# Retention attention and a two-layer MLP on one core: the MLP products in exact 12-bit pieces (three one-pass products) in place of Strassen on fp32, with half of the weights resident and two rounds over the token blocks

## The chip, the cores and the metric

The kernel runs on one core of a Trainium2 chip. The metric is the device time of one execution in microseconds (us); the kernel before takes 1010.7 us (median of three runs, 1009.96 to 1012.33). The engines are named as in the profile: PE is the matrix engine (PEld its weight loads), DVE the vector engine, ACT the scalar engine, POOL the GpSimd engine, SP the queue that issues most transfers. SBUF is the on-chip working memory, PSUM the small memory that PE writes into.

## The reference

Attention with decay for 8 batches and 8 heads, 576 positions, head size 64; its output, as 4608 tokens of 512 numbers, goes through a two-layer MLP with a PReLU between the layers.

```python
scores = q @ k^T / sqrt(64)
ret    = scores * Dmat                 # Dmat[i, j] = gamma_h ** (i - j) for i >= j, else 0
x      = (ret @ v) -> 4608 x 512
h = x @ w_in                           # 512 -> 2048
g = maximum(h, 0) + alpha * minimum(h, 0)
out = g @ w_out                        # 2048 -> 512, float32
```

The weights w_in and w_out reach the chip as float64 and are turned into float32 there. All products have to be good to fp32.

## The kernel before

Tokens are taken in 18 blocks of 256. The 2048 hidden channels are 8 units of 256. One unit of one block is the step that is repeated: h for 256 tokens and 256 channels, the PReLU, and that unit's share of the output. Blocks 0 and 1 use plain products while the weights still arrive (16 plain units); the other 16 blocks use Strassen's seven products of half-size operands (128 Strassen units). All matrices are fp32. Attention for a pair of heads is worked into the gaps between units: 28 pairs in this way, and the first batch in a form of its own at the start.

```python
def plain_unit(kb, i):                       # blocks 0 and 1
    for cc in range(NCC):                    # NCC = 4
        for x in range(2):
            nc.tensor.matmul(ph[:, x], w_in[...], xb[kb][:, cc], ...)      # L426, 256 columns
    ...
def mlp_unit(kb, i):                         # blocks 2 to 17
    for n, (m, o, l, r) in enumerate((... seven products ...)):
        for cc in range(2):
            nc.tensor.matmul(ph[m][:, o], w_in[i // UST][:, l, i % UST, cc], r[:, cc], ...)  # L470, 128 columns
    nc.scalar.copy(g[:, 7], ph[0][:, 2])
    for o, x0, x1 in (... four sums ...):
        nc.vector.tensor_tensor(out=o, in0=x0, in1=x1, op=ALU.add)         # L481, reads PSUM
    for m in range(2):
        nc.vector.tensor_scalar(g[:, 4 + 2 * m:6 + 2 * m], ..., ALU.min, ALU.mult)   # L484
    nc.vector.scalar_tensor_tensor(out=g[:, 0:4], ..., op0=ALU.max, op1=ALU.add)     # L486, both inputs in SBUF
    for o, x0, x1, op in (... four sums of g ...):
        nc.vector.tensor_tensor(out=g[:, o, :], in0=g[:, x0, :], in1=g[:, x1, :], op=op)   # L492, both in SBUF
    ...
def mlp_out(...):
    for n, (x, y) in enumerate(PROD):        # seven products
        nc.tensor.matmul(acc[kb][n // 2][:, n % 2, :], g[:, x, :], w_out[i][:, y, :], ...)  # L388, 256 columns
```

The weights stay on chip with their Strassen sums. Each piece of a weight (128 rows of 512 numbers; 32 pieces) is converted once from float64 while the plain blocks run. The intermediate c lies in PSUM.

```python
def piece_in(n):
    nc.scalar.activation(a, hi.bitcast(FP32), ACTF.Abs)
    nc.scalar.activation(lo, lo.bitcast(UINT32), ACTF.Copy, scale=2.0 ** -29)
def piece_out(n):
    c = ps_h.tile([P, 2, HM], INT32, tag="psh1", ...)                      # PSUM
    nc.vector.tensor_scalar(c.bitcast(FP32), a, HI_MIN, HI_MAX, ...)       # L307
    nc.vector.tensor_scalar(c, c, 3, 0x3FFFFFF8, ...)                      # L310
    nc.vector.scalar_tensor_tensor(out=dst, in0=hi, ..., in1=c, ...)       # L312
    nc.gpsimd.tensor_tensor(out=dst, in0=dst, in1=lo, op=ALU.add)          # L314
```

For a pair of heads ("joint", "pair_front", "running_sums", "pair_values") PE makes scores and states, DVE scales and masks the scores (four instructions, L636) and forms the running sums (L588 to L594), ACT copies the sums and q into the operands of the last product, POOL scales q (L531).

Of the kernel before, what the change touches and what calls it, by code (L numbers as in the profile page):

```python
# [10 lines left out]
FP32 = mybir.dt.float32  # L11
INT32 = mybir.dt.int32
UINT32 = mybir.dt.uint32
# [5 lines left out]
def kernel(  # L19
# [20 lines left out]
    NB = S // 32  # L40
# [3 lines left out]
    HM = DM // 2  # L44
    TB = 2 * P
    NKB = NTOK // TB
    NST = 4
    UST = NU // NST
    NRING = 6
# [3 lines left out]
    assert NPAIR == NCC and DM == 512 and NU % NST == 0 and TB % C == 0 and NB == 18  # L53
# [3 lines left out]
    wraw = ctx.enter_context(tc.tile_pool(name="wraw", bufs=3))  # L57
    ring = ctx.enter_context(tc.tile_pool(name="ring", bufs=1))
    xcomb = ctx.enter_context(tc.tile_pool(name="xcomb", bufs=2))
    nat = ctx.enter_context(tc.tile_pool(name="nat", bufs=2))  # L60
    attn = ctx.enter_context(tc.tile_pool(name="attn", bufs=1))
    mlp = ctx.enter_context(tc.tile_pool(name="mlp", bufs=3))
# [9 lines left out]


# [18 lines left out]


# [6 lines left out]

    def load_head(t, src, b, h):
        nc.sync.dma_start(t, src[b, h].rearrange("(j t) d -> t j d", t=C))

    def load_pair(n):
        b, c = pairs[n]
        kx, qx, kn = [nat.tile([P, S], FP32, tag=t, name=f"{t}_{n}") for t in ("kx", "qx", "kn")]
        kx, qx = [t.rearrange("p (n r) -> p n r", r=32) for t in (kx, qx)]  # L110
        kn = kn.rearrange("p (j d) -> p j d", d=D)
        vn = nat.tile([P, 2, NJ, D], FP32, tag="vn", name=f"vn_{n}")
# [5 lines left out]
        for h2 in range(2):  # L118

            nc.scalar.copy(vn[half(h2), h2, 0], zero[half(h2)])  # L120
# [3 lines left out]


    w_in = [wpool.tile([P, 7, UST, 2, P], FP32, tag=f"wi{i}", name=f"w_in{i}")
            for i in range(NST)]


    w_out = [wpool.tile([P, 7, HM], FP32, tag=f"wo{i}", name=f"w_out{i}") for i in range(NU)]  # L130


# [4 lines left out]

    def room(i, s0, n):
        return w_out[i][:, s0:s0 + n].rearrange("p s f -> p (s f)")
# [3 lines left out]
    part = [[room(i + 3 * (x % 2), 4 * (x // 2), 2 if x == 2 else 4).rearrange(  # L146
        "p (m h d) -> p m h d", h=H, d=D) for i in (2, 3, 4)] for x in range(2)]
    part.append([room(i, 4, 2).rearrange("p (m h d) -> p m h d", h=H, d=D) for i in (2, 3, 4)])
    sums = [[room(i, s0, 1).rearrange("p (c d) -> p c d", d=D) for i, s0 in x] for x in (
        ((5, 4), (5, 5), (5, 6), (6, 4)), ((6, 5), (6, 6), (7, 4), (7, 5)), ())]  # L150
    carry = [None] + [room(i, 6, 1).rearrange("p (c d) -> p c d", d=D) for i in (2, 7)]
# [28 lines left out]
    zero = const.tile([P, D], FP32, name="zero")  # L180
    nc.gpsimd.memset(zero, 0.0)
# [29 lines left out]
    th = const.tile([P, 4, H], FP32, name="th")  # L211
    nc.vector.scalar_tensor_tensor(out=tp[:, 0, 0], in0=pf[:, 1], scalar=float(D) ** -0.5,
# [5 lines left out]
    nc.vector.tensor_scalar(tp[:, 1], tp[:, 1], float(D) ** -0.5, None, ALU.mult)  # L218
# [3 lines left out]
    nc.vector.tensor_scalar(th[:, 0], pf[:, 1], float(D) ** -0.5, None, ALU.mult)  # L222
    nc.vector.reciprocal(pf[:, 1], pf[:, 1])
    nc.vector.tensor_tensor(out=th[:, 1], in0=pf[:, 1], in1=th[:, 2], op=ALU.mult)
    nc.vector.reciprocal(th[:, 3], th[:, 2])
# [4 lines left out]
    tabv = const.tile([P, NPAIR], FP32, name="tabv")  # L230
    for h2 in range(2):
        hd = slice(h2 * D, (h2 + 1) * D)
        nc.vector.tensor_copy(tabv[half(1 - h2)], th[half(1 - h2), 1, h2:H:2])
        nc.vector.tensor_copy(gch[hd, 0], th[hd, 2, h2:H:2])
        nc.vector.tensor_scalar(tabx[hd, :, 0], pf[hd, 0, h2:H:2], float(D) ** -0.5, None,
                                ALU.mult)
        nc.vector.scalar_tensor_tensor(out=tabx[hd, :, 1], in0=dif[hd, 5, h2:H:2], scalar=1.0,
                                       in1=tabx[hd, :, 0], op0=ALU.add, op1=ALU.mult)
    for i in range(2):
        nc.vector.tensor_tensor(out=gch[:, i + 1], in0=gch[:, i], in1=gch[:, i], op=ALU.mult)  # L240

    win32 = moe_w_in.bitcast(INT32).rearrange("(c p) (x f two) -> c p x f two", p=P, x=2, two=2)
# [784 lines left out]
```

## Time and profile before

| | before |
|---|---|
| time, median of three | 1010.7 us |
| profiled span | 1008.5 us |
| PE busy in 0 to 25 us, 25 to 50 us | 16.87, 23.81 us |
| DVE busy in 75 to 100 us, in 100 us from 300 us on | 22.88, 80.98 us |
| POOL busy in 125 to 150 us, in 100 us from 300 us on | 19.09, 9.10 us |
| moved between memory and chip | 64.30 MB, mean 64 GB/s |

How to read the profile: every instruction has a start and an end on its engine. Rows of groups give a count, the total busy time and the mean of one instruction. PE's instructions overlap (the end of one is modelled and reaches into the next), so a mean of PE is no rate; the distance from one start to the next is. An fp32 matmul shows as two records. In rows of the timeline, the first number is the start and the second the length of a run of like instructions.

### The profile page before, as it was taken

Reading aid. Unit: us, or ns where it says so; the run is one execution under the profiler, and the core shown is the slowest. Engines: PE = TensorE matmul, PEld = TensorE weight load, DVE = VectorE, ACT = ScalarE, POOL = GpSimd, SP = SyncE. Lnnn points to the kernel's source line nnn. Section 1 sums busy time; section 2 is a strip of 40 time slices with the busy share of each in tenths; the row PEclk is TensorE's granted clock in tenths of the full one; section 3 lists DMA queues with packets and bytes.
Section 4 is the critical chain, followed back from the end, with each engine's and each line's share of the span. In section 5 each row is a group of like instructions: output and inputs, shape, how many; then the busy total and the mean of one; then the engine's idle time right before and its main releaser. Section 6 shows DMA issues by size and latency. Waiting matters only on the chain.

```text
span 1008.5 us, 23133 instructions
## 1 busy us (share of the span) xinstructions
PE 995.2 (99%) x9389; PEld 891.9 (88%) x9389; DVE 773.4 (77%) x2086; ACT 267.3 (27%) x605; POOL 179.0 (18%) x201
## 2 busy tenths in 40 slices
PE   6999999999999999999999999999999999999998
PEld 5666668999999999999999999999999999999997
DVE  7769968887878778687777788878788776666665
ACT  5656652322222222022022121222222210000000
POOL 5656674210200020100020000200010001010000
PEclk9999999999999999999999999999999999999999
DMA  9986744232322222031122222323222000000000
GB/s 236 252 194 150 182 74 109 49 72 48 69 48 65 53 42 63 13 69 31 40 48 51 40 52 44 70 48 69 48 43 52 13 22 1 22 1 22 1 22 22
DMA packets 229595, 64.30 MB, mean 64 GB/s; under 512 B 214368, under 2 KB 223088, under 8 KB 229488
## 3 DMA queue, kind: packets, MB, share of 16 engines
q1 hardware_dynamic: 227088, 62.02, 27.4%
q8 instruction: 74, 1.21, 0.5%
q10 hardware_dynamic: 2400, 0.79, 0.4%
q14 instruction: 33, 0.27, 0.1%
HBM read 53.35 MB, written 9.44 MB: 62 GB/s over the span
## 4 chain that ended last, share of the span: by engine, by line
PE 98%; DMA 1%; issue 0%; DVE 0%; ACT 0%; SPq 0%; DVEq 0%
PE ph L470 40%; PE po L388 38%; PE ph L426 6%; PE po L405 6%; PE pv L652 3%; PE ps L616 1%; PE ps L622 1%; DMA w_out<-in_k_dram 1%; PE pv L966 1%; PE pt L695 0%; PE ps L714 0%; PE pv L773 0%; PE ps L559 0%; PE pu L734 0%; PE pu L577 0%
## 5 line engine op out<-in xcount | busy, mean ns | idle before, releaser
L388 PE MATMUL po<-w_out,g 128*128 128x256 f32 x1792 | 408.1, 379 | 0.0
L388 PEld LDWEIGHTS po<-w_out,g 128*128 128x128 f32 x1792 | 330.7, 190 | 39.7
L481 DVE TENSOR_TENSOR g<-ph,g 128x256 f32<-128x256 f32 (+1 forms) x512 | 187.0, 386 | 134.0 <-PE ph L470 67.7
L470 PE MATMUL ph<-xb,w_in 128*128 128x128 f32 x2048 | 272.7, 276 | 0.0
L470 PEld LDWEIGHTS ph<-xb,w_in 128*128 128x128 f32 x2048 | 257.1, 192 | 7.4 <-issue 0.5
L470 PE MATMUL ph<-xt,w_in 128*128 128x128 f32 x1536 | 213.3, 275 | 0.0
L470 PEld LDWEIGHTS ph<-xt,w_in 128*128 128x128 f32 x1536 | 192.1, 192 | 0.0
L476 ACT COPY g<-ph 128x128 f32<-128x128 f32 x128 | 34.1, 266 | 404.4 <-PE ph L470 391.9
L492 DVE TENSOR_TENSOR g<-g 128x128 f32<-128x128 f32 x512 | 129.4, 293 | 7.0
L531 POOL TENSOR_TENSOR qx<-qx,tabx 128x576 f32<-128x576 f32 x28 | 32.7, 1168 | 353.2 <-DMA qx<-in_q_dram 180.1
L486 DVE SCALAR_TENSOR_TENSOR g<-g 128x512 f32<-128x512 f32 x128 | 89.8, 701 | 3.0
L484 DVE TENSOR_SCALAR g<-g,alpha 128x256 f32<-128x256 f32 x256 | 85.8, 377 | 3.7
L405 PE MATMUL po<-w_out,g 128*128 128x512 f32 x128 | 58.6, 599 | 0.8 <-DVE g L442 0.8
L426 PE MATMUL ph<-xb,w_in 128*128 128x256 f32 x256 | 58.6, 383 | 0.0
L663 ACT COPY xb<-pv 128x256 f32<-128x256 f32 (+3 forms) x84 | 23.2, 315 | 126.5 <-PE pv L652 126.5
L426 PEld LDWEIGHTS ph<-xb,w_in 128*128 128x128 f32 x256 | 47.9, 190 | 9.3 <-issue 2.4
L600 ACT COPY vn<-su 64x512 f32<-64x512 f32 x56 | 34.5, 616 | 78.3 <-DVE su L594 77.9
L636 DVE SCALAR_TENSOR_TENSOR mt<-ps,th,mask 64x256 f32<-64x256 f32 x96 | 46.4, 483 | 2.2
L456 POOL TENSOR_TENSOR xt<-xb 128x256 f32<-128x256 f32 x16 | 11.6, 727 | 196.9 <-PE ph L470 196.9
L405 PEld LDWEIGHTS po<-w_out,g 128*128 128x128 f32 x128 | 23.4, 190 | 24.4 <-issue 22.8
L629 DVE SCALAR_TENSOR_TENSOR mt<-pv,th,mask 64x64 f32<-64x64 f32 x48 | 13.6, 283 | 40.2 <-ACT xb L663 39.8
L536 ACT ACTIVATE vn<-vn,tabv 64x576 f32<-64x576 f32 x56 | 43.2, 772 | 1.8 <-DMA vn<-in_v_dram 0.5
(136 smaller groups left out, 737.9 us busy)
## 6 DMA issues: line engine op xcount, KB each, us to landing
out_dram<-osb SPq DMA_DIRECT2D x34, 256.0 KB, 2.1
kx<-in_k_dram SPq DMA_DIRECT2D x112, 72.0 KB, 2.5
qx<-in_q_dram SPq DMA_DIRECT2D x112, 72.0 KB, 2.9
vn<-in_v_dram SPq DMA_DIRECT2D x56, 144.0 KB, 3.3
kn<-in_k_dram SPq DMA_DIRECT2D x56, 144.0 KB, 3.8
raw<-in_moe_w_in_dram SPq DMA_DIRECT2D x24, 256.0 KB, 4.4
raw<-in_moe_w_out_dram SPq DMA_DIRECT2D x10, 512.0 KB, 4.5
w_in<-in_moe_w_out_dram SPq DMA_DIRECT2D x6, 512.0 KB, 5.6
```

What stands on the lines that cost most here:

```text
L388: nc.tensor.matmul(acc[kb][n // 2][:, n % 2, :], g[:, x, :], w_out[i][:, y, :], start=(i == 0 and n % 2 == 0), stop=(i == NU - 1 and (n % ...
L405: nc.tensor.matmul(acc[kb][m], g[:, 2 * x + m], w_out[i][:, 2 * x:2 * x + 2].rearrange("p x f -> p (x f)"), start=(i == 0 and x == 0), sto ...
L426: nc.tensor.matmul(ph[:, x], w_in[i // UST][:, cc // 2 * 2 + x, i % UST, cc % 2], xb[kb][:, cc], start=(cc == 0 and x == 0), stop=(cc == N ...
L470: nc.tensor.matmul(ph[m][:, o], w_in[i // UST][:, l, i % UST, cc], r[:, cc], start=(n in (0, 3) and cc == 0), stop=(n in (2, 6) and cc == ...
L476: nc.scalar.copy(g[:, 7], ph[0][:, 2])
L481: nc.vector.tensor_tensor(out=o, in0=x0, in1=x1, op=ALU.add)
L484: nc.vector.tensor_scalar(g[:, 4 + 2 * m:6 + 2 * m], g[:, 2 * m:2 * m + 2], 0.0, alpha[:, fc:fc + 1], ALU.min, ALU.mult)
L486: nc.vector.scalar_tensor_tensor(out=g[:, 0:4].rearrange("p x t -> p (x t)"), in0=g[:, 0:4].rearrange("p x t -> p (x t)"), scalar=0.0, in1 ...
L492: ins = nc.vector.tensor_tensor(out=g[:, o, :], in0=g[:, x0, :], in1=g[:, x1, :], op=op)
L536: nc.scalar.activation(vn[x, h2], vn[x, h2], ACTF.Copy, scale=tabv[x, c:c + 1])
L600: nc.scalar.copy(vn[half(h2), h2, 1:], su[half(h2)])
L636: nc.vector.scalar_tensor_tensor(out=mt[to, h2, p2:NJ - 1:2], in0=ps[p2][half(x), 0], scalar=th[to, 3, h:h + 1], in1=mask[to, None, :].to_ ...
```

## The change

The change replaces the fp32 products. A float32 number has 24 significant bits; it is cut into an upper piece and a lower piece of 12 bits, and a third number d is a combination of the two. The product of two numbers is then made from three products of pieces (upper by upper, lower by lower, d by d) in place of the four of a full multiplication. The pieces are given to PE in the type float32r[...]; with 12 bits each the products are meant to be exact. Two PSUM banks hold the sums, and the result is (1 + 2^-12) times the first less the second.

What follows from it: activations and weights take three times their room, so only four of the eight weight units lie on chip. The blocks are gone over twice: units 0 to 3 first, then 4 to 7; around the middle, blocks 14 to 17 change to and fro while the second half of the weights comes in. Between the rounds a block's x and its half sum are kept in memory off chip. In the attention part, four scale-and-mask instructions leave DVE (scale on ACT, mask on POOL), and four copies leave ACT and become transfers. Some tiles of the pairs now have one buffer in place of two.

The step that repeats is now a cell: one unit of one block. 18 blocks by 8 units are 144 cells, in 42 visits of 2 or 4 cells each.

```diff
+PIECE = mybir.dt.float32r
+    ONE = 1.0 + 2.0 ** -12
+    BELOW = 1.0 - 2.0 ** -13
...
-    wraw = ctx.enter_context(tc.tile_pool(name="wraw", bufs=3))
+    wraw = ctx.enter_context(tc.tile_pool(name="wraw", bufs=2))
-    nat = ctx.enter_context(tc.tile_pool(name="nat", bufs=2))
+    nat = ctx.enter_context(tc.tile_pool(name="nat", bufs=1))
...
-            c = ps_h.tile([P, 2, HM], INT32, tag="psh1", name=f"wc_{at}")
+            w = wraw.tile([P, DM], INT32, tag="wc", name=f"wc_{at}")
+            nc.vector.tensor_scalar(w.bitcast(FP32), a, HI_MIN, HI_MAX, ALU.max, ALU.min)
+            nc.vector.tensor_scalar(w, w, 3, 0x3FFFFFF8, ...)
+            nc.vector.scalar_tensor_tensor(out=w, in0=hi, scalar=-0x40000000, in1=w, ...)
+            nc.gpsimd.tensor_tensor(out=w, in0=w, in1=lo, op=ALU.add)
+    def piece_lim(n):
+            nc.scalar.mul(h, w, BELOW * 2.0 ** -12)
+            nc.vector.scalar_tensor_tensor(out=l, in0=to[:, 0], scalar=-4096.0, in1=w, ...)
+            nc.gpsimd.tensor_tensor(out=d, in0=to[:, 0], in1=to[:, 1], op=ALU.subtract)
+    def split(to, w):
+        nc.scalar.mul(piece(to[0]), w, BELOW)
+        nc.vector.scalar_tensor_tensor(out=piece(to[2]), in0=to[0], scalar=ONE, in1=w,
+                                       op0=ALU.mult, op1=ALU.subtract)
+        nc.gpsimd.tensor_tensor(out=piece(to[1]), in0=w, in1=to[0], op=ALU.subtract)
...
+    def prepare(vis):                    # once a visit: x kept or fetched, then split, 128x1024
+            nc.sync.dma_start(x_kept[kb], x...)   or   nc.sync.dma_start(x..., x_kept[kb])
+        split(vis["x"], x)
+    def mm_h(cell):
+        for f in range(2):
+            for n, (b, l) in enumerate(((0, 0), (1, 2), (0, 1))):
+                for cc in range(NCC):
+                    nc.tensor.matmul(ph[:, b], piece(w_at[u, cc // 2][...]), piece(x[l][:, cc]), ...)
+    def post_h(cell):
+        for f in range(2):
+            nc.scalar.copy(gc[:, f], ph[:, 1])
+            nc.vector.scalar_tensor_tensor(out=gb[:, f], in0=ph[:, 0], scalar=ONE, in1=gc[:, f], ...)
+        nc.scalar.activation(gc, gb, ACTF.Relu, scale=-1.0)
+        nc.scalar.activation(gb, gb, ACTF.Relu)
+        for f in range(2):
+            nc.vector.scalar_tensor_tensor(out=gb[:, f], in0=gc[:, f], scalar=nalpha[...], in1=gb[:, f], ...)
+        split([g[:, l] for l in range(3)], gb)
+    def mm_o(cell):
+        for m in range(2):
+            for f in range(2):
+                for b, l in ((0, 0), (0, 1), (1, 2)):
+                    nc.tensor.matmul(acc[2 * m + b], piece(g[:, l, f, m * P:(m + 1) * P]),
+                                     piece(w_at[u, 2 + f][:, l]), ...)      # 512 columns
+    def evacuate(vis):                   # once a visit
+        for m in range(2):
+            nc.scalar.copy(t, acc[2 * m + 1])
+            nc.vector.scalar_tensor_tensor(out=o, in0=acc[2 * m], scalar=ONE, in1=t, ...)
+            if vis["has"]:
+                nc.gpsimd.tensor_tensor(out=o, in0=o, in1=vis["o"][:, m], op=ALU.add)
+            nc.sync.dma_start(out[...] if vis["final"] else o_kept[kb][:, m], o)
+    order = [(0, (0, 1)), (1, (0, 1, 2, 3)), (0, (2, 3))]
+    order += [(kb, (0, 1, 2, 3)) for kb in range(2, 14)]
+    order += [(14, (0, 1)), (15, (0, 1)), (16, (0, 1)), (17, (0, 1, 2, 3)), (16, (2, 3)),
+              (15, (2, 3)), (14, (2, 3, 4, 5)), (15, (4, 5)), (16, (4, 5)), (17, (4, 5, 6, 7)),
+              (16, (6, 7)), (15, (6, 7)), (14, (6, 7))]
+    order += [(kb, (4, 5, 6, 7)) for kb in range(14)]
...
-            nc.scalar.copy(vn[half(h2), h2, 1:], su[half(h2)])
+            nc.sync.dma_start(vn[half(h2), h2, 1:], su[half(h2)])
-            nc.scalar.copy(mt[half(h2), h2].rearrange("p j s -> p (j s)"), qT[half(h2)])
+            nc.sync.dma_start(mt[half(h2), h2].rearrange("p j s -> p (j s)"), qT[half(h2)])
+                nc.scalar.activation(mt[to, h2, p2:NJ - 1:2], ps[p2][x, 0], ACTF.Copy, scale=...)
+            nc.gpsimd.tensor_tensor(out=mt[to, h2, 0:NJ - 1], ..., op=ALU.mult)
...
+    for cell in cells[4:]:
+        prepare(cell["vis"])
+        mm_h(cell)
+        post_h(cell)
+        pend.append(cell)
+        if len(pend) > 2:
+            mm_o(pend.pop(0))
```

Of the weight pieces, 16 are converted in the first six cells (units 0 to 3), and 16 (units 4 to 7) between the last cell of block 17's first visit and the cell (17, 5). The pairs of batch 1 fall in cells 4 to 7, those of the other batches in the cells up to about number 58.

## The prediction

> **What bounds the kernel now.** I read the page first: the busy shares, and the chain of work that ended last.
>
> ```profile
> PE 995.2 (99%) x9389; PEld 891.9 (88%) x9389; DVE 773.4 (77%) x2086; ACT 267.3 (27%) x605; POOL 179.0 (18%) x201
> ...
> PE 98%; DMA 1%; issue 0%; DVE 0%; ACT 0%; SPq 0%; DVEq 0%
> ```
>
> PE is never waiting except for some 13 us (1008.5 less 995.2), which lie in the first 50 us and in the last few. So the time is the sum of PE's work, and I need its rates. They come from PE's timeline late in the run, where one Strassen unit of a block is seen from the start of its output products to the start of the next unit's.
>
> ```profile
> 899.92 3.19 PE L388 MATMUL po<-w_out,g 128*128 128x256 f32 x14
> 902.94 1.05 PE L470 MATMUL ph<-xb,w_in 128*128 128x128 f32 x8
> 903.83 1.06 PE L470 MATMUL ph<-xt,w_in 128*128 128x128 f32 x8
> 904.73 1.06 PE L470 MATMUL ph<-xb,w_in 128*128 128x128 f32 x8
> 905.62 0.61 PE L470 MATMUL ph<-xt,w_in 128*128 128x128 f32 x4
> 906.07 2.11 PE L388 MATMUL po<-w_out,g 128*128 128x256 f32 x9
> ```
>
> From start to start: 14 records of 256 columns take 3.02 us, 0.2157 us each; 28 records of 128 columns take 3.13 us, 0.1118 each. An fp32 matmul is two records, so 256 columns cost 0.431 us, 1.68 ns a column. [...] A unit is 6.15 us, 128 of them 787 us. The plain units take 6.88 us (63.21 to 70.09 in the same view), 16 of them 110. The rest of PE's 995 us, 98 us, is attention (the first batch about 22, a pair about 2.4).
>
> Next the other engines, since the change gives them work: groups by shape, the time of one instruction being the last number before the second bar.
>
> ```profile
> L486 DVE SCALAR_TENSOR_TENSOR g<-g 128x512 f32<-128x512 f32 x128 | 89.8, 701 | 3.0
> L442 DVE SCALAR_TENSOR_TENSOR g<-g,nalpha,ph 128x256 f32<-128x256 f32 x32 | 13.9, 476 | 17.4 <-ACT ph L432 17.4
> L310 DVE TENSOR_SCALAR wc<-wc 128x512 int32<-128x512 int32 x32 | 22.4, 699 | 1.1
> L324 POOL TENSOR_TENSOR w_in<-w_in 128x512 f32<-128x512 f32 x16 | 20.4, 1273 | 7.0 <-DVE g L492 6.7
> L296 ACT ACTIVATE wa<-raw 128x512 f32<-128x512 f32 x22 | 14.8, 674 | 2.7 <-DMA raw<-in_moe_w_in_dram 1.9 <-DMA raw<-in_moe_w_out_dram 0.7
> ```
>
> Last, what DVE and POOL do to each other. Both timelines at two places; the first pair has DVE reading two SBUF operands, the second has one of DVE's operands in PSUM.
>
> ```profile
> 329.48 1.25 DVE L492 TENSOR_TENSOR g<-g 128x128 f32<-128x128 f32 x1
> ...
> 17.20 0.69 DVE L312 SCALAR_TENSOR_TENSOR w_in<-raw,wc 128x512 int32<-128x512 int32 x1
> ```
>
> ```profile
> 329.44 1.15 POOL L531 TENSOR_TENSOR qx<-qx,tabx 128x576 f32<-128x576 f32 x1 [14.98 <-DVE g L492]
> ...
> 16.81 2.53 POOL L314 TENSOR_TENSOR w_in<-w_in,raw 128x512 int32<-128x512 int32 x2
> ```
>
> L492 normally takes 0.29 us; started 0.04 us after a POOL instruction it ended 0.14 us after that instruction did. L312, with wc in PSUM, took its usual 0.69. So DVE with two SBUF operands and POOL take turns. The same happens to L484 (SBUF to SBUF, one operand), 1.36 us at 171.12 in place of a usual 0.35.
>
> [...]
>
> **The change part by part.** *PE.* A cell has 24 products of 256 columns and 12 of 512[...]: 24 x 0.1118 + 12 x 0.2157 = 5.27 us, 144 cells 759 us. [...] That takes 787 + 110 − 759 = 138 us away. Attention's 98 us stay. PE's work is 857 us.
>
> *DVE per cell:* two L442-like (0.43 start to start), two SBUF ones of 256 (about 0.41), the split of 512 (0.70): 2.4 us. Per visit 1.23 for x and 2 x 0.70 to evacuate. A visit of four cells: 12.2 us beside 21.1 of PE. *ACT* about 13. A pair: DVE 4.5 us (6.5 now, less four L636 at 0.48). *POOL:* 1.25 per cell, about 2.35 for x, 2 x 1.25 where a half sum is added (24 of 42 visits), two more 1.25 per pair.
>
> *Port time*, what POOL and two-operand DVE hold in turns. I count POOL whole and DVE at its length less 0.15 us (L492 ended 0.14 after POOL). Cell: 1.25 + 2 x 0.27 + 0.54 = 2.33. Visit: 2.35 + 1.07 = 3.4, and 2.5 with a half sum. Pair: 3.8. Weight piece: POOL 2 x 1.25, DVE 2 x 0.54 and two tensor_scalars, which now write SBUF, about 0.27 each: 4.1. The intermediate in PSUM kept this off the port before.
>
> *Second round* (four cells, one visit): port 9.3 + 3.4 + 2.5 = 15 of 21.1 us. Hidden. *First round*, cells 8 to 58: 50 cells with 23 pairs, 26 us of PE a visit with 2 pairs; port 20.5, DVE 21.5 plus blocked time, say 5. Nearly level; I take 12 us of PE waits in all.
>
> *Start, up to cell 8:* 16 pieces 66, first-batch scaling on POOL 17, eight cells 19, four visits' x 14, five pairs 19, a half sum 2.5: 137 us of port, beginning at about 10 us. PE's work there is 22 + 8 x 5.27 + 12 = 76. Cell 8 would start near 140, so PE idles about 60 us, where it idled 9 before.
>
> ```profile
> 0.00:25.00 25.00, 16.87 (x333) 13.46 (x333) 18.24 (x62) 13.93 (x28) 14.10 (x25) 1.00 0.96 235
> 25.00:50.00 25.00, 23.81 (x410) 17.38 (x411) 18.10 (x32) 15.23 (x29) 16.27 (x15) 1.00 0.98 254
> ```
>
> Here (busy time of PE, PEld, DVE, ACT, POOL in stretches) DVE is already busy 18 of 25 us with half as many pieces per PE time.
>
> *Middle, 15 cells with the other 16 pieces:* port 66 + 15 x 2.33 + 6 x 3.4 + 5 x 2.5 = 134 us beside 79 of PE. DVE alone is about 91. Two cells of products wait in reserve, and an overlap of forms that do not hold the port is possible: 38 us of the 55 are lost. *End:* copy, two adds and a transfer after the last matmul, 5 us.
>
> Sum: 857 + 60 + 12 + 38 + 5 = 972 us. The transfers (x and half sums off chip, about 47 MB, and copies on chip) double the 64 MB, some 130 GB/s beside 254 seen; they stay hidden.
>
> **Rivals.** (A) PE remains the bound as before: the engines' idle halves absorb everything, the start costs 25 us, the middle nothing: about 890. For it: the second round has room, and the scheduler interleaves DVE finely. Against: the two stages above carry more port than PE time. (B) Port and DVE bound the first round too, because blocked DVE exceeds 26 us a visit and pairs with one buffer wait for their chain (sums, transfer, transposes, some 12 us against 8 us between pairs in cells 4 to 7): start 75, middle 55, first round 50: 1040. For it: DVE's order is fixed, so a blocked instruction holds up those behind it. (C) [...] the weight load does not hide behind 256 columns. PEld is busy 88% now[...]. At 0.135 us in place of 0.112 it adds 80 us (1050)[...]. I give C one in twelve.
>
> **Range and chances.** A and B lie 80 us below and 70 above my sum; the start and the middle, 98 us together, are the terms that I trust least. Range 905 to 1040. Faster by over 2% needs less than 990.5: the sum clears it by 18 us only, but the order of cells and the moves off DVE look balanced by trial, so 0.66. Within 2%: 0.19. Slower: 0.15.
>
> **What would show it.** Right: in the second round 5.27 us a cell and PE full; starts of 256-column products 0.11 us apart, one record each; DVE's two-operand forms well over 0.7 us on average; PE idle about 60 us before cell 8 and 38 in the middle, with DVE or POOL named as releasers. Wrong: PE full from 50 us on (A), gaps spread through all of the first round (B), or spacings over 0.12 us (C).

## The result, and the profile after

The changed kernel takes 1219.6 us (median of four runs, 1218.6 to 1221.5) against 1010.8 us on the same chip: 1.206 times the time before, 95% interval 1.205 to 1.208. It is slower by 209 us; 972 had been predicted, and 905 to 1040 as the range.

The page of the kernel after: busy time by engine, then two of the rows of 40 slices (each 30 us wide), PE's busy tenths and the clock that was granted to it.

```profile
PE 1014.9 (83%) x8813; PEld 873.0 (72%) x8813; DVE 786.8 (65%) x1306; ACT 608.1 (50%) x1219; POOL 670.2 (55%) x414
PE   5672757789788987887888876869999999999998
PEclk8775777899898999998999999989999999999999
```

Before, PE was busy for 99% of the span at a mean clock of 0.999. Now it is full only in the last third, and in many of the slices in which it is not, its clock is at 5 to 8 tenths. "Busy 1014.9 us" is therefore no measure of work: products at a lower clock last longer (at a granted 0.50, shown below, those of 512 columns stand about 0.45 us apart, and 0.23 at 1.00).

The busy times by stage show it. I cut the run where certain cells begin: cell 8 (end of the start), cell 58 (last pair done; it begins at 663 us, and the stretch below is cut at 660), cell 79 (second half of the weights on chip). Stretches of the kernel after; columns: stretch and its length, busy time of PE, PEld, DVE, ACT and POOL with counts, granted clock, DMA share, GB/s.

```profile
0.00:187.00 187.00, 110.57 (x1489) 91.36 (x1489) 117.26 (x206) 81.42 (x159) 104.05 (x89) 0.74 0.52 126
187.00:660.00 473.00, 391.12 (x4194) 323.73 (x4186) 269.76 (x520) 234.04 (x498) 217.95 (x135) 0.93 0.50 117
660.00:839.00 179.00, 141.01 (x782) 120.36 (x781) 156.07 (x199) 95.22 (x182) 125.67 (x70) 0.91 0.34 114
839.00:1218.70 379.70, 372.21 (x2366) 337.52 (x2364) 243.75 (x383) 197.41 (x382) 222.55 (x122) 1.00 0.22 74
```

In the long second stretch, the first round with its 23 pairs, none of the other engines is near full: DVE 57%, POOL 46%, ACT 49%. Only in the third, where weights are converted, is one of the others at 87%. Set beside the terms of the prediction:

| stage | predicted, us | measured, us |
|---|---|---|
| A, up to cell 8 | 140 | 187 |
| B, cells 8 to 57 (50 cells, 23 pairs) | 331 (50 x 5.27 + 23 x 2.4 + 12) | 476 |
| C, cells 58 to 78 (conversion) | 149 (21 x 5.27 + 38) | 176 |
| D, cells 79 to 143 and the end | 348 (65 x 5.27 + 5) | 380 |

The second round gives the rate of the new products. PE's timeline of the kernel after (start, length of the run of like instructions, count at the end):

```profile
1001.88 2.91 PE L396 MATMUL po<-w,g 128*128 128x512 f32 x12
1004.63 3.04 PE L358 MATMUL ph<-lx,w 128*128 128x256 f32 x24
1007.50 2.91 PE L396 MATMUL po<-w,g 128*128 128x512 f32 x12
```

From start to start a cell is 5.62 us: 24 products of 256 columns in 2.87 (0.1197 each), 12 of 512 in 2.75 (0.229 each). Each is one record, as predicted (3456 and 1728 of them on the page), but a record takes 7% longer than that of an fp32 product of half as many columns did (0.1118 and 0.2157). That one record is one pass, as the title has it, is not shown by any run.

What the vector engines do now, from the page's groups of the kernel after (busy time and mean ns between the two bars, then idle time ahead of them):

```profile
L321 POOL TENSOR_TENSOR g<-gb,g 128x512 fp32r<-128x512 f32 x144 | 250.3, 1738 | 267.5 <-ACT g L318 226.3
L376 DVE SCALAR_TENSOR_TENSOR gb<-gc,nalpha,gb 128x256 f32<-128x256 f32 x288 | 209.1, 766 | 78.6 <-ACT gb L373 77.6
L319 DVE SCALAR_TENSOR_TENSOR g<-g,gb 128x512 fp32r<-128x512 f32 x144 | 122.5, 851 | 68.2 <-ACT g L318 67.5
```

L376 takes 0.48 us undisturbed and 0.77 on average, L319 0.69 and 0.85: two-operand forms do stand while POOL works, as L492 did before (1.25 us in place of 0.29). Two of L376 take 2.92 us at 1004.69, where an instruction of POOL runs from 1003.49 to 1006.93, and 0.88 at 1011.17, where none runs. L370, which has an operand in PSUM, never takes over 0.43 in its 288. The question is whether that is what costs the time.

**A reckoning from the starts.** For each stage I took the distances between the starts of PE's products. Up to the second round's spacing (0.1197 and 0.2298 us; 0.05 for attention's small products) a distance counts as work; what goes beyond counts as slow products while the distance is below some 2.5 spacings, and as a wait above. It is good to some 12 us in a column, since attention's share is rough and the line between a slow product and a short wait can be drawn elsewhere; the sum of the two hardly moves.

| stage of the kernel after | work, us | slow products, us | waits, us |
|---|---|---|---|
| A | 70 | 29 | 83 |
| B | 327 | 54 | 95 |
| C | 118 | 15 | 43 |
| D | 369 | 2 | 2 |

So B lost some 150 us and A 110; C lost 58, and the second round nothing.

The column of slow products is not the clock alone. The clock record of this trace has two values, 1.0 and 0.5. In B, 476 us at a mean of 0.93, some 68 us ran at half clock, in twelve stretches of 3.4 to 10.2 us; that can cost at most 34 us. Counted from the starts inside these stretches it cost about 23 us in B, 20 in A and 12 in C. The rest of the column is mostly short delays at full clock.

What a loss in B looks like: PE's timeline of the kernel after (in brackets the idle time ahead, and who ended it), then ACT's and POOL's over the same cell.

```profile
301.65 3.14 PE L358 MATMUL ph<-lx,w 128*128 128x256 f32 x24
305.23 0.70 PE L526 MATMUL pv<-mt,vn 128*64 128x64 f32 x4 [0.44 <-issue]
309.37 0.80 PE L396 MATMUL po<-w,g 128*128 128x512 f32 x1 [3.44 <-ACT g L318]
311.21 5.02 PE L396 MATMUL po<-w,g 128*128 128x512 f32 x11 [1.05 <-POOL g L321]
```

```profile
304.82 0.37 ACT L369 COPY gc<-ph 128x256 f32<-128x256 f32 x1 [0.39 <-PE ph L358]
306.33 0.63 ACT L372 ACTIVATE gc<-gb 128x512 f32<-128x512 f32 x1 [1.13 <-DVE gb L370]
307.05 0.63 ACT L373 ACTIVATE gb<-gb 128x512 f32<-128x512 f32 x1
308.68 0.63 ACT L318 ACTIVATE g<-gb 128x512 fp32r<-128x512 f32 x1 [1.01 <-DVE gb L376]
```

```profile
309.45 1.70 POOL L321 TENSOR_TENSOR g<-gb,g 128x512 fp32r<-128x512 f32 x1 [3.91 <-ACT g L318]
```

The hidden products of a cell run at 301.65, and the next output products on PE are those of the same cell: the scheduler that fixes the order of the instructions has used up the two cells in reserve that the program's text keeps. From the end of the last hidden product, at 304.79, the second half goes through copy, difference (DVE, with running sums of the pair in between), two relus, PReLU and the three pieces, and the last piece is done at 311.15: 6.4 us. PE has nothing but the start of a pair's last products to put there, and stands for 3.44 us and again for 1.05. After that, eleven products take 5 us, about 0.45 each in place of 0.23: the clock has been halved (granted 0.50 from 309.3 to 316 us). So a wait of 4.5 us costs about 7.

### The profile page after: what moved, and what is told of

It is laid out like the page before. It is cut to its first block, busy times and chain, and to the rows that moved or that the text cites. A ratio compares the mean times of both kernels' runs of the same rounds, so it can differ in the third digit from the quotient of the medians.

```text
span 1218.7 us, 22971 instructions
## 1 busy us (share of the span) xinstructions
PE 1014.9 (83%) x8813; PEld 873.0 (72%) x8813; DVE 786.8 (65%) x1306; ACT 608.1 (50%) x1219; POOL 670.2 (55%) x414
## 4 chain that ended last, share of the span: by engine, by line
PE 33%; DVE 12%; ACT 6%; issue 5%; POOL 4%; DMA 2%; SPq 0%; POOLq 0%; ACTq 0%; DVEq 0%
PE po L396 16%; PE ph L358 15%; DVE gb L376 4%; POOL g L321 2%; ACT mt L512 1%; DVE gb L370 1%; ACT g L318 1%; PE pv L526 1%; DVE o L409 1%; DVE w L312 1%; DVE wc L295 1%; DVE su L468 1%; ACT lx L318 1%; POOL wc L300 1%; ACT gb L373 1%
## 5 line engine op out<-in xcount | busy, mean ns | idle before, releaser
L396 PE MATMUL po<-w,g 128*128 128x512 f32 x1728 | 465.3, 417 | 73.7 <-POOL g L321 34.4
L358 PE MATMUL ph<-lx,w 128*128 128x256 f32 x3456 | 469.5, 293 | 59.4 <-DVE gb L370 38.2
L358 PEld LDWEIGHTS ph<-lx,w 128*128 128x128 f32 x3456 | 448.6, 199 | 83.2 <-DVE gb L370 49.1
L396 PEld LDWEIGHTS po<-w,g 128*128 128x128 f32 x1728 | 333.0, 200 | 164.5 <-POOL g L321 47.7
L321 POOL TENSOR_TENSOR g<-gb,g 128x512 fp32r<-128x512 f32 x144 | 250.3, 1738 | 267.5 <-ACT g L318 226.3
L376 DVE SCALAR_TENSOR_TENSOR gb<-gc,nalpha,gb 128x256 f32<-128x256 f32 x288 | 209.1, 766 | 78.6 <-ACT gb L373 77.6
L319 DVE SCALAR_TENSOR_TENSOR g<-g,gb 128x512 fp32r<-128x512 f32 x144 | 122.5, 851 | 68.2 <-ACT g L318 67.5
L370 DVE SCALAR_TENSOR_TENSOR gb<-ph,gc 128x256 f32<-128x256 f32 x288 | 115.4, 417 | 28.1 <-ACT gc L369 17.7
L369 ACT COPY gc<-ph 128x256 f32<-128x256 f32 x288 | 102.4, 367 | 55.7 <-PE ph L358 53.9
L373 ACT ACTIVATE gb<-gb 128x512 f32<-128x512 f32 x144 | 91.0, 632 | 7.6
```

The costliest lines, as they stand in the source:

```text
L319: nc.vector.scalar_tensor_tensor(out=piece(to[2]), in0=to[0], scalar=ONE, in1=w, op0=ALU.mult, op1=ALU.subtract)
L321: nc.gpsimd.tensor_tensor(out=piece(to[1]), in0=w, in1=to[0], op=ALU.subtract)
L358: nc.tensor.matmul(ph[:, b], piece(w_at[u, cc // 2][:, l, (cc % 2 * 2 + f) * P: (cc % 2 * 2 + f + 1) * P]), piece(x[l][:, cc]), start=(n = ...
L369: nc.scalar.copy(gc[:, f], ph[:, 1])
L370: nc.vector.scalar_tensor_tensor(out=gb[:, f], in0=ph[:, 0], scalar=ONE, in1=gc[:, f], op0=ALU.mult, op1=ALU.subtract)
L373: nc.scalar.activation(gb, gb, ACTF.Relu)
```

## The experiments

Two theories. **Order and latency**: PE comes to products whose operands are late, because in the fixed order of each engine a short step that PE waits for stands behind long ones. **Load**: DVE and POOL lack the time, since POOL's instructions and DVE's of two SBUF operands take turns. The recorded texts call what they hold in turns the port; the runs show the turns (the 2.92 us above), not what lies behind them. A third thing to settle is the rate of the products. Below, A, B and C are the stages of the tables; for the kernel after they are 187, 476 and 176 us. Times with an interval are from two to four executions, the others from one; executions of one version lay up to 0.5% apart.

### The source's order, and the subtraction of the split on DVE

The kernel lets the scheduler reorder what follows cell 3. First run: the order of the program's text to the end. Second: in the split of x and of g, the subtraction moves from POOL to DVE. Third: both. Fourth: PE reads the upper two bytes of each piece as bf16 (so the sums lack the lower bits; the work is otherwise the same).

```diff
 e_order
     operands(NPAIR)
-    ordered.close()
-    tc.no_sync_barrier()
     ...
     while pend:
         mm_o(pend.pop(0))
+    ordered.close()
 e_dve_split
-        nc.gpsimd.tensor_tensor(out=piece(to[1]), in0=w, in1=to[0], op=ALU.subtract)
+        nc.vector.tensor_tensor(out=piece(to[1]), in0=w, in1=to[0], op=ALU.subtract)
 e_bf16
-        nc.tensor.matmul(ph[:, b], piece(w_at[...]), piece(x[l][:, cc]), ...)
+        nc.tensor.matmul(ph[:, b], half_piece(w_at[...]), half_piece(x[l][:, cc]), ...)   # bitcast to bf16, [:, 1::2]
```

> Edit: the changed kernel with its engines kept in the order of the source to the end (the scheduler is no longer allowed to move instructions after the first four cells). In the changed kernel the output products of a cell stand right behind that cell's own hidden products for most of cells 8 to 57, where the source has them two cells later. Order theory (PE meets products whose g is not formed yet because of that order): cells 8 to 57 take about 350 us in place of 473, the granted clock there goes from 0.93 to about 1, total about 1100 us. Port theory (POOL and two-operand DVE instructions holding each other up set the pace of the first round): cells 8 to 57 stay above 440 us, total 1180 to 1220 us.

> Edit: the changed kernel with the subtraction of the split (lower pieces of g and x, 144 of 128x512 and 42 of 128x1024) moved from POOL to DVE, so POOL falls from 670 to about 280 us busy. Port theory: DVE's g instructions fall back from 0.77 and 0.85 us to about 0.42 and 0.70, cells 8 to 57 fall below 400 us, total about 1100 us. Order theory: the waits of PE in cells 8 to 57 change their releaser from POOL to DVE but stay; total 1170 to 1230 us.

> Edit: both of the edits before together. Order theory: within 25 us of the kernel in source order alone, about 1090 us. Port theory: within 25 us of the one with the subtraction on DVE alone. If both act: lower than either by over 25 us.

> Edit: the changed kernel with PE reading only the upper 16 bits of each piece, as bf16 with a step of two, in place of float32r (so the products are no longer those of the reference; counts, columns and addresses are the same). A cell of the second round takes 5.62 us in the changed kernel, where 5.27 were predicted. Theory of the type (float32r, four bytes an element, costs it): about 5.27 us a cell or less. Theory of the fixed cost [...]: 5.55 to 5.65 us a cell.

Measured: e_order 1375 us (ratio 1.361, interval 1.356 to 1.365), with A 197, B 552, C 203, and the second round 40 longer. e_dve_split 1188 us (1.175, 1.169 to 1.181), with A 186, B 452, C 153, and the second round 18 longer. e_order_dve 1388 us (1.373, 1.368 to 1.379), B 538, C 203, and the second round 68 longer. e_bf16 1203 us, B 471.

The same instructions in another order change B by 76 us, but not in the direction that the theory of order had given (350 for B); e_order's total is not load's either (1180 to 1220). In the text's order PE waits for the running sums; PE's waits in e_order, 197 to 750 us (total, times, longest):

```profile
PE pv L526 <- DMA vn<-su: 66.1, 30, 9.4
```

The program defers the sums by a cell, they then go by a transfer into the operand of the pair's last product, and PE stands ahead of that product, with others behind it in its order. The scheduler's order is better than this, not good. (In it, 17 of B's 50 cells have their output products right behind their own hidden products, not most of them as I wrote ahead of e_order; 18 keep one cell between, 15 two.) Giving POOL's subtraction to DVE takes 24 us off B in the scheduler's order, which can change with the edit, and 14 in the text's, which does not: POOL and its turns with DVE count for something, but for a sixth of B's loss at most.

e_bf16 asks where the 0.35 us a cell come from: the type, or a fixed cost of each product whatever its type. Its PE timeline in the second round, and its weight loads from the groups by shape:

```profile
1002.72 2.86 PE L399 MATMUL po<-w,g 128*128 128x512 bf16 x12
1005.42 2.88 PE L361 MATMUL ph<-lx,w 128*128 128x256 bf16 x24
1008.14 2.86 PE L399 MATMUL po<-w,g 128*128 128x512 bf16 x11
```

```profile
L361 PEld LDWEIGHTS <-w 128*128 128x128 bf16 x3456 | 341.4, 100 | 173.9 <-issue 58.1 <-POOL w L317 12.8 <-ACT w L314 10.3
```

A cell is 5.42 us here; the weight load has gone from about 200 ns to 100. So 0.20 of the 0.35 go with the type, which is neither of the two figures expected. The other 0.15 stay with two-byte pieces too, and what they are I have not found.

### One suspected cost taken out at a time

e_no_pairs leaves out the attention of batches 2 to 7, 23 of the 28 pairs (blocks 4 and up take the x of earlier blocks, by the same transfers). e_raw leaves out the conversion of the weights: the pieces are made from the upper word as it comes. e_act gives the pairs' four copies back to ACT. e_su gives the running sums a buffer of their own. e_free keeps all instructions of the pairs but takes away what they wait for: operands are those of the first pair, and sums go to memory that nobody reads.

```diff
 e_no_pairs
-    for b in range(2, B):
+    for b in range(2, 2):
     ...
 e_raw
-            nc.scalar.activation(a, hi..., ACTF.Abs); nc.scalar.activation(lo, ...)      # piece_in
-            nc.vector.tensor_scalar(w...); (w...); nc.vector.scalar_tensor_tensor(out=w, ...)
-            nc.gpsimd.tensor_tensor(out=w, in0=w, in1=lo, op=ALU.add)                     # piece_mid
+            stage_c.append((at, hi.bitcast(FP32), t))
 e_act
-            nc.sync.dma_start(vn[half(h2), h2, 1:], su[half(h2)])
+            nc.scalar.copy(vn[half(h2), h2, 1:], su[half(h2)])
-            nc.sync.dma_start(mt[half(h2), h2]..., qT[half(h2)])
+            nc.scalar.copy(mt[half(h2), h2]..., qT[half(h2)])
 e_su
-        su = attn.tile([P, S], FP32, tag="kT", ...)
+        su = attn.tile([P, S], FP32, tag="su", ...)
 e_free
-        return kT, qT
+        return kept[0]                                                # the first pair's
     ...
-            nc.sync.dma_start(vn[half(h2), h2, 1:], su[half(h2)])
+            nc.sync.dma_start(nowhere[half(h2)], su[half(h2)]...)
```

> Edit: the changed kernel without the attention of batches 2 to 7 (23 of 28 pairs are left out; blocks 4 to 17 take the kept x of blocks 2 and 3 in its place, so the output is not the reference's). Everything else of a cell is as it was. Pair theory (the pairs, whose chain of scores, sums, transfers and transposes is as long as the two cells between them, cause the loss in cells 8 to 57): cells 8 to 57 take 5.7 to 6.2 us each, 280 to 310 us in all in place of 473, at a clock of 1, total about 1020 to 1060 us. MLP theory (the cells alone, with DVE and POOL blocking each other, cannot keep PE full in the first round): cells 8 to 57 take over 350 us, total above 1090 us.

> Edit: the changed kernel with the conversion of the weights from float64 left out (two ACT, three DVE and one POOL instruction less for each of 32 pieces; the upper halves of the float64 words go into the split as they are, so the output is not the reference's). Theory of the prediction [...]: cell 8 starts 30 to 45 us earlier than at 187, cells 58 to 79 take 135 to 150 us in place of 179, total about 1140 us. Chain theory (the start waits for the pairs and the order of instructions): cell 8 starts less than 15 us earlier; total above 1180 us.

> Edit: one part of the change undone: the four copies of a pair (q into the operand of the last product, the running sums into its other operand) are ACT copies again (about 0.62 and 0.67 us each) and not transfers (3 to 4 us to landing). Pair theory: the chain of a pair gets 2 to 3 us shorter and with it each of 28 pairs, total 1140 to 1170 us. Theory of loaded engines (ACT, DVE and POOL set the pace): 2.6 us more on ACT for each pair, no gain, total 1200 to 1260 us.

> Edit: the running sums of a pair get a buffer of their own in place of the one of the transposed k, so the transposes of the next pair no longer wait for the transfer of the sums. Pair theory, if this shared buffer is the long link: 1 to 3 us less for each of 28 pairs, total 1140 to 1190 us. If the link is elsewhere (sums, transfer, products of g): within 15 us of 1219.

> Edit: the changed kernel with every instruction of the pairs kept, but what they wait for taken away: the transposes of pairs 5 to 31 write a spare buffer (the scores use those of pair 4), and the running sums go from there to memory in place of the operand of the last product, which keeps zeros (so the output is not the reference's). PE, DVE, ACT, POOL and the transfers do as much as before. Waits theory (a pair costs 8.4 us in cells 8 to 57 because its chain from one pair to the next is longer than the work between): those cells fall from 476 to 340 to 390 us, total 1080 to 1130 us. Load theory (the pairs' instructions on DVE, ACT and POOL, and what these block of each other, cost it): above 430 us, total above 1170 us.

Measured: e_no_pairs 1016 us, B 283, A 182, C 170. e_raw 1170 us, A 169, B 478, C 141. e_act 1357 us (1.343, 1.337 to 1.349), B 623. e_su 1253 us, B 505. e_free 1317 us, B 587.

Stretches of e_no_pairs in the first round, columns as above:

```profile
200.00:300.00 100.00, 97.42 (x619) 87.99 (x618) 65.33 (x104) 54.05 (x105) 49.69 (x25) 1.00 0.15 52
300.00:400.00 100.00, 100.00 (x645) 91.40 (x644) 61.25 (x106) 53.78 (x104) 45.97 (x23) 1.00 0.14 51
```

Without pairs PE is full and its clock whole, with DVE at 61 to 65%, a higher share than the 57% of the kernel after. The split, the turns of POOL and DVE and the evacuations of a cell are no limit in the first round by themselves. The pairs are what costs: (476 − 283) / 23 = 8.4 us each, where PE's own work on one is about 2.4.

e_raw takes 35 us off C, where DVE was nearly full, and e_dve_split 23, though it gives DVE more to do: in that stage DVE, with its waits for POOL, is a bound. It holds for the scheduler's order; in the text's, the same move of the subtraction left C at 203. e_raw takes only 18 off A, though I had counted 66 of A's 137 us of port time as conversion: the start is not bound by these turns. e_no_pairs leaves A nearly as it was, since the five pairs of cells 4 to 7 stay in it.

e_act, e_su and e_free each give the program fewer waits or no more of them, and each made B longer. In e_free the scheduler put the pair's last product right behind the scores, so that PE waited 68.2 us in B for the masks. These three changed the order of everything at once; they say how much hangs on the order, and nothing of the buffers or copies that they were meant to test. (e_free's figure lies where load had it, but for this reason it does not speak for load.)

### The order by hand

So that only the order differs, the rest keeps the text's order through cell 57, which is mine to set. e_front: the running sums follow their states at once, q and k are fetched a pair earlier, the sums have a buffer of their own.

```diff
-        later.append(lambda: pair_sums(vn, running_sums(n, ps[0][:, 1], ps[1][:, 1])))
+        pair_sums(vn, running_sums(n, ps[0][:, 1], ps[1][:, 1]))     # ahead of the scores' scaling
     ...
+        if n == 57:
+            ordered.close()
```

> Edit: the pairs of the changed kernel put in another order, which is then kept through cell 57: running sums and their transfer straight behind a pair's first products, ahead of its scores on ACT; the transposes of the next pair ahead of the next cell's PReLU, k scaled after it, q and k fetched a pair earlier, a buffer of their own for the sums; output products two cells behind, as in the source. No work is added or left out. Waits theory: cells 8 to 57 take 350 to 410 us (source order as it was: 552; scheduler's order: 476), total 1090 to 1150 us. Load theory: above 450 us, total above 1190 us.

Measured: 1256 us (1.242, 1.239 to 1.246), B 506: 46 better than the text's order, 30 worse than the scheduler's, and on the side that load had given (above 450). The trace shows why: DVE, POOL and PE at one place in e_front.

```profile
452.94 5.20 DVE L328 SCALAR_TENSOR_TENSOR lx<-lx,xb 128x1024 fp32r<-128x1024 f32 x1 [2.48 <-ACT lx L327]
458.06 0.77 DVE L468 STREAM_TRANSPOSE kT<-kx 128x576 f32<-128x576 f32 x1
458.76 0.73 DVE L468 STREAM_TRANSPOSE qT<-qx 128x576 f32<-128x576 f32 x1
459.42 0.71 DVE L379 SCALAR_TENSOR_TENSOR gb<-ph,gc 128x256 f32<-128x256 f32 x2
```

```profile
450.97 2.65 POOL L528 TENSOR_TENSOR mt<-mt,mask 64x512 f32<-64x512 f32 x2 [3.48 <-ACT mt L526]
453.59 2.36 POOL L330 TENSOR_TENSOR lx<-xb,lx 128x1024 fp32r<-128x1024 f32 x1
455.92 1.14 POOL L454 TENSOR_TENSOR qx<-qx,tabx 128x576 f32<-128x576 f32 x1
```

```profile
459.85 4.63 PE L367 MATMUL ph<-lx,w 128*128 128x256 f32 x24 [4.84 <-DVE gb L379]
```

The split of x on DVE (1.23 us undisturbed) stood through three of POOL's instructions in a row (the second mask, the subtraction of the split, the scaling of q; the last ends at 457.06) and took 5.20, to 458.14; two transposes followed; only then came L379, which empties the banks of the hidden products. PE stood for 4.84 us. In e_front these waits for gb make 48.6 us of B, and another 39.2 are for a small step of the pair (mt, L519) that sits in the same banks and stood behind the running sums.

Four runs act on that reading. e_front2 reorders only: the small step goes ahead of the sums, the transposes go into DVE's gap while ACT does the two relus, x is split in a cell without a pair. e_front3 also gives the masks back to DVE, e_front4 also the split's subtraction. e_mask gives the masks to DVE in the scheduler's order.

```diff
 e_front2, on e_front
+        (extra's scalar_tensor_tensor moved ahead of pair_sums)
         nc.vector.scalar_tensor_tensor(out=gb[:, f], in0=ph[:, 0], ...)   # post_h
+        while cell["n"] > 4 and later:
+            later.pop(0)()                                                # transposes of the next pair
         nc.scalar.activation(gc, gb, ACTF.Relu, scale=-1.0)
-            if kb not in xb or NPAIR * (ready[kb] + 1) in done:
+            if (...) and (n > 57 or not todo.get(n) or cell["last"]):
 e_mask, and e_front3 on e_front2
-                nc.scalar.activation(mt[to, h2, p2:NJ - 1:2], ps[p2][x, 0], ACTF.Copy, scale=...)
-            nc.gpsimd.tensor_tensor(out=mt[to, h2, 0:NJ - 1], ..., op=ALU.mult)
+                nc.vector.scalar_tensor_tensor(out=mt[to, h2, p2:NJ - 1:2], in0=ps[p2][x, 0],
+                    scalar=pf[to, 1, h:h + 1], in1=mask[...], op0=ALU.mult, op1=ALU.mult)
 e_front4, on e_front3: the edit of e_dve_split
```

> The same instructions as the kernel after, in an order of my own through cell 57: as e_front, but the last chunk's small DVE step, which frees a bank of the hidden products, goes ahead of the running sums; the transposes of the next pair stand in DVE's gap while ACT does the two relus; the scaling of q follows at once; and x of the next visit is split in a cell without a pair. Theory of order: the two largest waits of e_front (48.6 us for gb, 39.2 us for mt) mostly go, cells 8 to 57 fall from 506 to 400-440 us, total 1150-1190. Theory of load: the waits only move, the stage stays at 480-510, total 1230-1260.

> e_front2 with the scores scaled and masked on DVE out of PSUM again (four instructions)[...]. Theory of order: cells 8 to 57 at 370-410 us, total 1110-1160 (ratio 1.10 to 1.15). Theory of load: 480 or more, total above 1220.

> e_front3 with the subtraction of the split on DVE in place of POOL. Of the port theory: another 20-30 us off cells 8 to 57 and 20 off the middle, as between the first two runs (24 and 23). Of order alone: cells 8 to 57 as in e_front3 within 10 us, and the middle 20 less[...]. Total 1090-1140; the second round may cost 18 us more, as it did before.

> One part of the change undone: the scores of a pair are scaled and masked by four DVE instructions out of PSUM again (as L636 of the kernel before), in place of four of ACT (0.49 each) and two of POOL (1.33 each); the scheduler keeps its freedom. Theory of order (g of a cell is late because the pair's ACT work stands ahead of it, and DVE waits behind POOL's masks): cells 8 to 57 fall from 476 to 430-460 us, unless the scheduler finds a worse order, and the total to 1175-1205. Theory of load [...]: DVE gains 2 us a pair and loses 2.65 of blocking by POOL, so no change within 10 us: 1210-1230.

Measured: e_front2 1190 us, B 440. e_front3 1194 us (1.181, 1.178 to 1.183), B 442. e_front4 1210 us (1.196, 1.194 to 1.198), B 470, C 159. e_mask 1225 us, B 480.

Moving a few instructions took B from 506 to 440, at the upper edge of what the theory of order had said of e_front2 (400 to 440) and far from the 480 or more of load; the two waits aimed at fell from 87.8 to 13.1 us. Beyond that order had promised too much: with the masks off POOL, e_front3 stayed at 442 where 370 to 410 was expected, and e_mask came out as load had it, unchanged. Neither theory had e_front4: relieved of the split as well, POOL was hardly used, and B lost 28 us, most likely because the subtraction now stands in DVE's order, ahead of steps that PE waits for (PE's waits for L379 rose from 11.1 to 20.8 us). So POOL's turns with DVE are not what holds B. In C, where the other engines are full, e_front4 has the 20 us that were expected.

B stays 110 us above its work in e_front3, though. My reckoning puts 69 to waits and 42 to slow products there, and the last two runs ask whether the slow ones come from the waits. The largest waits left there are 17.2 us for the evacuation of a visit's sums (DVE, o) and 13.3 us for the scaled k of a pair (ACT); no run takes these out.

### Filling the waits

e_front3 with products of a matrix of zeros, added to the output sums (which they leave as they are): 8 behind the pair in 17 cells, or 16 in each of 37 cells.

```diff
+    def warm(cell):
+        for _ in range(0 if cell["last"] else 8):                    # e_warm2: 16
+            nc.tensor.matmul(acc[1][0:C], piece(zr), piece(w_at[cell["u"], 2][:, 0]),
+                             start=False, stop=False, skip_group_check=True)
```

> e_front3 with 8 products of a zero matrix (512 columns each, 1.8 us at full rate, adding nothing to the sums) behind the pair in 17 of the cells 8 to 57: 31 us more of work, laid where PE often waits. Cells 8 to 57 took 442 us in e_front3, 42 of them by products at doubled spacing. If waits lower the clock: the granted clock of 190 to 630 us rises from 0.91 to 0.94 or more, the doubled spacings cost under 30 us, and the stage stays at 430-450. If the slow products are a fixed cost: the clock stays at 0.91, and the stage takes 455-475.

> 16 products of the zero matrix in each of 37 cells, with or without a pair: 136 us more of work, more than all of PE's waits in this stage (69). If waits lower the clock: waits and doubled spacings both nearly vanish (clock 0.98 or more), and the stage takes 331 + 136 + some 15 = 480 us, only 40 more than without them. If the slow products are a fixed cost: about 40 us of them stay, clock 0.93, 510 or more.

Measured: e_warm 1194 us, B 444; e_warm2 1250 us, B 500. The stretch from 190 to 630 us in e_front3, e_warm and e_warm2, in this order (columns as above):

```profile
190.00:630.00 440.00, 378.10 (x4224) 332.31 (x4224) 291.50 (x615) 193.77 (x407) 156.61 (x88) 0.92 0.54 123
```

```profile
190.00:630.00 440.00, 395.44 (x4360) 337.35 (x4360) 293.93 (x612) 191.08 (x404) 156.16 (x87) 0.96 0.54 123
```

```profile
190.00:630.00 440.00, 429.13 (x4213) 346.88 (x4214) 262.63 (x541) 171.02 (x355) 142.18 (x79) 0.99 0.49 112
```

| B of | work | slow products | waits | sum |
|---|---|---|---|---|
| e_front3 | 332 | 42 | 69 | 442 |
| e_warm | 361 | 30 | 53 | 444 |
| e_warm2 | 465 | 17 | 18 | 500 |
| e_no_pairs | 275 | 3 | 6 | 283 |

Some 31 us of added products (17 x 8 x 0.23) cost 2 us, and 136 cost 58: PE really had nothing to do there, and when it is kept busy the clock comes back (0.92, 0.96, 0.99). e_warm2 missed the 480 that I had given for it by 20, and 17 us of slow products remain, most of them at full clock: of B, 71 us ran at half clock in e_front3, 40 in e_warm and 13 in e_warm2. This lies on the side of the waits as the cause. Work on zeros is no gain by itself.

No version beats the kernel before: the best of those that leave nothing out are e_dve_split at 1188 and e_front2 at 1190 us, and even without 23 of the pairs the time is 1016 us.

## Why the prediction was wrong, point by point

**PE's cell, 5.27 us: mis-sized.** One record a product was right, and so was the full PE of the second round. The step that failed is the working "24 x 0.1118 + 12 x 0.2157": I took for a new product the distance of one record of an fp32 product of half as many columns, an estimate that rested on no measured product of the new type. The runs show 0.1197 and 0.2298, 5.62 a cell, 0.35 x 144 = 50 us in all. Rival C had named a slower spacing, but at 0.135; the spacing stayed just short of the 0.12 that was to be its sign. Of the 0.35, 0.20 go with the type (e_bf16). Whether that is its weight load (200 ns against 100) is not shown: the loads of the fp32 products lasted 190 ns too.

**First round, "Nearly level; I take 12 us of PE waits in all": this is the step that failed most.** It lost 149 us (95 of waits, 54 of slow products). I compared the busy and port time of a visit with PE's 26 us and took what fits on average for hidden. The averages were not too low (DVE was busy for about 22 us a visit, blocked time included, where I had counted 26.5), and they did not matter. Each pair makes PE's fixed order depend on several short steps within a few us, and how late those come is set by what stands ahead of them: 552, 506, 476 and 440 us for almost the same instructions in four orders. POOL's turns with DVE are not the reason for most of it: without pairs, with all of the splits, PE is full, and with POOL's subtractions and masks moved to DVE (e_front4) B is no shorter. What the orders show is how far the loss moves, from 110 us above the work to over 200; that a better order would remove the last 110 is not shown.

Rival B foresaw that the first round would be bound and that pairs would do it, for a third of the size (50 us). Its reason, a chain through buffers that are one deep, is not shown: the runs meant for it changed the order as well. That stays open. Its other reason, that a blocked DVE instruction holds up those behind it, is what e_front's trace shows (5.20 us, and 4.84 us of PE).

**The clock: missing from the sum.** No term of mine said that products behind a wait can run at half rate (0.45 us in place of 0.23); the kernel before did not show it: its clock stayed at 1.00 in the first 50 us, where PE idled 9. By the granted clock it is worth about 55 us in A, B and C together (20, 23 and 12), and e_warm2 shows it going when the waits are filled.

**Start, cell 8 "near 140", bound by port time: right in kind, wrong in cause.** PE idles there as foreseen (83 us of waits for 60), and 29 us of slow products come on top, 20 of them by the half clock. But taking away the conversion moved cell 8 by 18 us only, so the 137 us of port time are not what sets it. Cells 4 to 7 with five pairs take 100 us of the 187, at a clock of about 0.7; the longest waits there are 11.2 us for the transposed q of a pair and 6.5 for running sums on their way by transfer. That looks like B, but the orders by hand, which begin with cell 4, left A at 186 to 190 us. What would shorten the start stays open.

**Middle, 38 us lost: mechanism right, size off.** It lost 58 (43 of waits, 15 of slow products). e_raw and e_dve_split took 35 and 23 off: in the scheduler's order DVE and its turns with POOL are a bound here, as argued.

**End 5, transfers hidden: right.** The run ends 5.7 us after the last product. Traffic doubled to 127 MB at 104 GB/s, and the second round, which fetches x and half sums all the time, has 2 us of waits.

**Chances.** The sum stood 18 us below the 2% line, on top of two stages that I trusted least; 0.15 for slower was too little for a change that makes ACT, DVE and POOL each take part in every cell between two steps of PE.

## What to carry to other kernels

Where PE is full because it needs little from others, a change that saves PE work but puts more short steps of other engines between its products must be judged by the order and latency of those steps within one repeat, not by busy shares: follow one cell with its pair from the last hidden product to the first product that needs its result, with everything that stands ahead on ACT, DVE and POOL. Add something to each wait of some us on PE, since the products behind it can run at half clock, as they did in twelve stretches of B: in the example above 2.4 us on 4.5, over the whole first round about 23 us on some 125 of waits and short delays. And measure one product of a new type before multiplying by five thousand.

## What the runs showed of the hardware that I had not expected

- Products of 12-bit pieces in float32r are 0.1197 us apart at 256 columns and 0.2298 at 512, with a weight load each of about 200 ns; the records of fp32 products were 0.1118 at 128 columns and 0.2157 at 256, with loads of about 190. With bf16 halves of the same bytes it is 5.42 us a cell in place of 5.62, and the load takes 100 ns.
- The granted clock dropped around waits of PE: in B of the kernel after it is 0.50 in twelve stretches of 3.4 to 10.2 us, and the output products shown at 311.21 are about 0.45 us apart in place of 0.23. The waits were of no one length: 3.44 us ended at 309.37, but in the 10 us before, four of the twelve stretches had a single idle time over 0.4 us, of 2.9 us (the one at 350 us, for example), and a fifth a single one of 1.75 us (at 251).
- DVE's instructions with two SBUF operands and POOL's took turns, and one of DVE's can lose to three in a row: in e_front 5.20 us for the 128x1024 split that takes 1.23 alone.
